# Two batches share one output chunk in a fused attention and gated FFN kernel, with a new instruction order

## The chip, the core and the metric

The kernel runs on one NeuronCore of a Trainium2 chip. The core has a matrix engine (TensorE, in the profile PE, with its weight loads as PEld), a vector engine (VectorE, DVE), a scalar engine (ScalarE, ACT), a general engine (GpSimd, POOL) and a queue engine that only issues DMAs (SyncE, SP). Each engine works through its own instructions strictly in the order in which they were written; semaphores make one engine wait for another. Results of TensorE go to PSUM, everything else on the chip lies in SBUF.

The metric is the device time of one execution in microseconds, as the median of several runs.

## The reference

Eight batches of 576 tokens, eight heads of 64. A causal attention with a forget gate comes first, and its output goes through a feed-forward layer with a gate made by a convolution over the tokens:

```python
scores = scale * np.matmul(q, k.transpose(0, 1, 3, 2))
cum = np.cumsum(np.log(np.clip(f, 0.0001, 1.0)), axis=-1)
decay = cum[:, :, :, None] - cum[:, :, None, :]
scores = np.where(causal, -1000000000.0, scores + decay)
attn = softmax(scores)                         # over the keys
x = np.matmul(attn, v)  -> (8, 576, 512)       # heads side by side
h = np.maximum(x @ w_in, 0.0)                  # 512 -> 1024
conv_out = sum over k of conv_w[k] * h shifted by k - 1 tokens
out = (h * sigmoid(conv_out)) @ w_out          # 1024 -> 512, float32
```

## The kernel before

**Tiles.** The attention is done in 16 half-batches (hb) of four heads, so hb 2b and 2b + 1 make batch b. 576 tokens are four blocks of 128 and a rest of 64. The feed-forward layer takes a batch at a time, in eight blocks (ff) of 128 hidden channels, with all 576 tokens as columns.

**Tasks.** Everything is written as small tasks with short names. `add` gives each its engine, the tasks it comes after, the buffers it takes and those it gives back. The string ORDER (one line, near the top of the file) lists all tasks; `plan.play` writes their instructions in just this order, so ORDER alone sets the order of every engine's queue. `name@ENGINE` picks the engine for tasks that may run on several. The names:

- `q` loads the transposed queries (side 0) or keys (side 1) of an hb with a transposing DMA (L179), into one of four buffers `qk`; hb 0 and 1 are loaded plainly (`ld`) and turned on PE (`tp`). `cl` is a pass over the loaded rows on VectorE (L185; for hb 0 and 1 it is the copy out of PSUM, L171/L173). `rw` puts the decay rows into them by two small DMAs (L201, L202). From hb 8 on `fi` does both with DMAs alone: a blank fill and the decay rows (L193, L195).
- `sd`, `so`, `st`: score matmuls of the diagonal blocks, the other blocks and the 64-token rest (L311, with a mask matmul L319 for hb under 8). `ed`, `eo`, `et`: their exponentials on ScalarE (L352, L369, L331). `md`, `mt`: masks on GpSimd from hb 8 on.
- `v` loads values, `va` casts them (L216, L218). `pv` multiplies probabilities and values (L388, L393); `n` and `m` divide by the sums on VectorE (L402, L404).
- `t` turns the result on PE and `tx` copies it out (L413, L416); for hb 11 to 15 `tx` is a transposing DMA on SP instead (L419).
- `f`: first layer (L428), `r`: relu on ScalarE (L438), `c`, `d`: the convolution on VectorE (L444, L446), `a`: tanh or sigmoid on ScalarE (L449), `g`: the gate on VectorE (L456, L454), which leaves the hidden layer in a buffer `hg`. `h` takes that buffer.
- `o`: second layer. A batch's output is made in chunks of 128 tokens x 512 columns, each 8 matmuls over ff (L463). The chunk of the last 64 tokens is made as two halves of 256 columns, which lie on PSUM partitions 0 to 63 and 64 to 127; that is 16 matmuls of 64 columns of weights (L467). `e` copies chunks out of PSUM to an output buffer `ob`, on ScalarE or VectorE (L473; L478 for the last batch), `s` stores it (L489, L493, L484).

**Buffers.** There are two `hg` buffers, three `ob` buffers (which also take in the weights w_in and w_out at the start, tasks `wi`, `wo`; `wic`, `woc` cast them) and four PSUM tiles `ps`. A task that takes a buffer waits for the task that gave it back.

**Order of the queues.** SP issues nearly all DMAs, in order; an issue that must wait (for a buffer, or as `fi` for the landing of `q`) holds all issues behind it. The same holds for a copy `e` on ScalarE or VectorE which waits for the store that frees its buffer.

The output matmuls before, with the half chunks in the else branch, are these:

```python
if c < 4:
    nc.tensor.matmul(ps[:, 512 * (c % 2):512 * (c % 2 + 1)], hg_of(b, ff)[:, 128 * c:128 * (c + 1)],
                     w_out_f16[:, ff, :], **kw)
else:
    for a in range(2):
        nc.tensor.matmul(ps[64 * a:64 * (a + 1), 0:256], hg_of(b, ff)[:, 512:576],
                         w_out_f16[:, ff, 256 * a:256 * (a + 1)], skip_group_check=True, **kw)
```

Of the kernel before, what the change touches and what calls it, by code (L numbers as in the profile page):

```python
# [7 lines left out]
FP32 = mybir.dt.float32  # L8
# [48 lines left out]
def kernel(  # L57
# [26 lines left out]
    RING, NP, NPT, NVA, NVF, NX, NRC, NXT, NHT, NU, NHG, NOB = 4, 6, 4, 4, 2, 2, 3, 2, 5, 4, 2, 3  # L84
    NPL = 2
    PAIRS = 2
    NCL = 8
    MASK_PE = (0, 1, 2, 3, 4, 5, 6, 7,)
    NPD, NP3 = 2, 2
    TURN_DMA = (11, 12, 13, 14, 15,)  # L90
    CUT, PER, NXB = 14, 7, 18
    VW = D + 2
    LATE = [(b, ff) for b in range(B) for ff in range(8) if b == 7 or b == 6 and ff >= 3]

    cpool = ctx.enter_context(tc.tile_pool(name="const", bufs=1))
    ctx.enter_context(tc.manual_schedule())
# [38 lines left out]
    hg_t = [cpool.tile([128, NFF, S], FP16, name=f"hg{t}") for t in range(NHG)]  # L135
# [547 lines left out]
```

## Time and profile before

| | |
|---|---|
| median of 3 runs | 248.52 us (247.74 to 249.3) |
| the profiled execution's own time | 248.12 us |
| its span (first to last instruction) | 246.4 us |
| TensorE busy | 229.4 us, 93% |
| ScalarE busy | 207.7 us, 84% |
| VectorE busy | 203.8 us, 83% |
| GpSimd busy | 52.1 us, 21% |
| granted TensorE clock | 1.00 throughout |

The span is what the profiler saw of the program; 1.7 us of the execution lie outside it. A busy time is the union of an engine's instructions; matmuls are pipelined, so the rows of PE overlap by some 0.16 us at their ends, and a wait shorter than that hides in a busy PE. Lines such as L428 are those of the program before; in the changed program the same code stands one to eight lines further down.

In the views quoted below, a stretch gives the busy time and the number of instructions for PE, PEld, DVE, ACT and POOL, then the granted clock, the DMA share and GB/s. A piece of the chain of waits gives its start, its length and what the run was held by. A timeline row gives start, length, engine, line, operation, tiles, and in brackets the idle time before it and what ended that.

### The profile page before, as it was taken

The numbers are of one execution on the slowest core, as the hardware profiler recorded it, in microseconds if no ns is written. First come the engines' busy times: TensorE is split into PE (matmuls) and PEld (weight loads), VectorE is DVE, ScalarE is ACT, GpSimd is POOL, SyncE is SP. The second block draws the span as 40 slices with busy tenths as digits, with TensorE's granted clock in tenths as the row PEclk, the third lists the DMA queues.
The fourth block names the chain that finished last, engine by engine and source line by source line (L and its number), as shares of the span: only waits on it lengthen the run. The fifth ranks groups of instructions, "written<-read, shape, count | busy, mean of one in ns | idle before, by whom it ended". The sixth has DMA issues, their size and how long they took to land.

```text
span 246.4 us, 6604 instructions
## 1 busy us (share of the span) xinstructions
PE 229.4 (93%) x2723; PEld 147.6 (60%) x2723; DVE 203.8 (83%) x325; ACT 207.7 (84%) x278; POOL 52.1 (21%) x79
## 2 busy tenths in 40 slices
PE   0798899988999999999999999999989999999993
PEld 0776686566655575586657755685656567445451
DVE  5635068999899999999899889989888889999940
ACT  2764978999989899999889999999989996688733
POOL 8020430011620050021511336030334320000000
PEclk9999999999999999999999999999999999999999
DMA  7999899999899999999999989999899960804335
GB/s 180 331 162 253 260 203 208 189 200 229 263 230 191 212 214 256 230 247 249 217 232 163 243 224 188 240 190 163 240 193 269 200 216 3 179 23 174 106 106 192
DMA packets 120849, 49.70 MB, mean 202 GB/s; under 512 B 109919, under 2 KB 111455, under 8 KB 120819
## 3 DMA queue, kind: packets, MB, share of 16 engines
q1 hardware_dynamic: 120573, 48.91, 92.6%
q8 instruction: 21, 0.34, 0.6%
q10 hardware_dynamic: 246, 0.37, 0.5%
q14 instruction: 9, 0.07, 0.1%
HBM read 21.11 MB, written 10.17 MB: 127 GB/s over the span
## 4 chain that ended last, share of the span: by engine, by line
PE 63%; DMA 13%; DVE 9%; SPq 7%; ACT 4%; issue 2%; ACTq 0%; DVEq 0%
PE ps L428 19%; PE ps L463 18%; PE ps L311 12%; PE ps L388 6%; DMA qk<-in_k_dram 5%; DVE u L446 3%; SPq L179 3%; DMA qk<-in_q_dram 3%; SPq L208 3%; PE ps L467 2%; DMA u<-in_f_dram 2%; PE ps L393 2%; DVE u L444 2%; DMA qk<-image 2%; PE ps L413 2%
## 5 line engine op out<-in xcount | busy, mean ns | idle before, releaser
L428 PE MATMUL ps<-xt,w_in_f 128*128 128x512 f16 (+1 forms) x512 | 69.7, 286 | 0.2 <-DMA xt<-xm 0.2
L369 ACT ACTIVATE pp<-ps 128x1024 f16<-128x1024 f32 x64 | 64.7, 1038 | 3.3 <-PE ps L311 2.1
L311 PE MATMUL ps<-qk 128*128 128x128 bf16 (+2 forms) x576 | 64.0, 240 | 2.9 <-ACT pp L352 0.8
L463 PE MATMUL ps<-w_out_f,hg 128*128 128x512 f16 x256 | 59.7, 379 | 0.0
L444 DVE SCALAR_TENSOR_TENSOR u<-ht,cwt 128x576 f32<-128x576 f16 x64 | 53.3, 846 | 2.2 <-ACT ht L438 2.0
L446 DVE SCALAR_TENSOR_TENSOR u<-ht,cwt,u 128x576 f32<-128x576 f16 x64 | 53.5, 850 | 0.6
L311 PEld LDWEIGHTS <-qk 128*128 128x128 bf16 x576 | 39.0, 98 | 22.0 <-issue 3.5
L449 ACT ACTIVATE hg<-u,cw 128x576 f16<-128x576 f32 x64 | 48.6, 782 | 3.9 <-PE ps L467 1.9
L428 PEld LDWEIGHTS <-w_in_f 128*128 128x128 f16 x512 | 34.2, 98 | 28.9 <-issue 0.5
L438 ACT ACTIVATE ht<-ps 128x576 f16<-128x576 f32 x64 | 41.2, 658 | 5.9 <-PE ps L428 5.1
L463 PEld LDWEIGHTS <-hg 128*128 128x128 f16 x256 | 23.8, 98 | 26.0 <-issue 0.6
L456 DVE SCALAR_TENSOR_TENSOR hg<-hg,ht 128x576 f16<-128x576 f16 x51 | 37.5, 760 | 0.2 <-ACT hg L449 0.2
L355 POOL TENSOR_SCALAR_AFFINE_SELECT pp<-pd 128x1024 f16<-128x1024 f32 x16 | 19.8, 1251 | 47.6 <-ACT pd L352 47.6
L404 DVE TENSOR_TENSOR xm<-ps,rc 128x896 f16<-128x896 f32 (+1 forms) x32 | 23.9, 752 | 1.0 <-DVE rc L402 0.2
L388 PE MATMUL ps<-va,pp 128*128 128x65 f16 x640 | 24.0, 193 | 0.3 <-ACT pp L369 0.3
L388 PEld LDWEIGHTS <-pp 128*128 128x128 f16 x640 | 22.2, 97 | 2.0 <-issue 0.5
L216 POOL CAST va<-vf 128x1024 f16<-128x1024 f32 x9 | 10.8, 1209 | 54.8 <-DMA vf<-in_v_dram 34.2
L352 ACT ACTIVATE pp<-ps 128x1024 f16<-128x1024 f32 x16 | 16.3, 1031 | 1.4 <-PE ps L316 0.8
L473 ACT COPY ob<-ps 128x1024 f32<-128x1024 f32 (+1 forms) x16 | 13.0, 810 | 5.0 <-PE ps L463 1.3
L352 ACT ACTIVATE pd<-ps 128x1024 f32<-128x1024 f32 x16 | 16.4, 1028 | 0.8 <-POOL pt L334 0.5
L402 DVE RECIPROCAL rc<-ps 128x14 f32<-128x14 f32 (+1 forms) x32 | 6.6, 206 | 11.7 <-PE ps L388 7.1
L319 PE MATMUL ps<-mask,ident 128*128 128x512 bf16 (+1 forms) x40 | 14.3, 358 | 1.6 <-ACT qk L171 1.0
(84 smaller groups left out, 187.7 us busy)
## 6 DMA issues: line engine op xcount, KB each, us to landing
vf<-in_v_dram SPq DMA_DIRECT2D x32, 256.0 KB
out_dram<-ob SPq DMA_DIRECT2D x14, 512.0 KB
qk<-blank SPq DMA_DIRECT2D x8, 540.0 KB
ob<-in_moe_w_in_dram SPq DMA_DIRECT2D x4, 512.0 KB
ob<-in_moe_w_out_dram SPq DMA_DIRECT2D x4, 512.0 KB
vf<-in_v_dram SPq DMA_DIRECT2D x8, 128.0 KB
out_dram<-ob SPq DMA_DIRECT2D x4, 256.0 KB
out_dram<-ob SPq DMA_DIRECT2D x15, 64.0 KB
```

The source lines that it names most:

```text
L311: nc.tensor.matmul(o, tk[:, h * S + k0:h * S + k0 + 128], tq[:, h * S + q0:h * S + q0 + n], start=first, stop=last and not by_matmul(hb, h))
L352: nc.scalar.activation(o, ps_of(f"sd{i}").rearrange("p (s c) -> p s c", s=2), AF.Exp, scale=SCALE)
L369: nc.scalar.activation(pair(i)[:, s, 512:1536], ps_of(f"so{i}.{s}"), AF.Exp, scale=SCALE)
L388: nc.tensor.matmul(ps[:, c:c + D + 1], block(hb, h, m, n), va[:, h, m, 0:D + 1], start=(m == 0), stop=(m == n))
L404: nc.vector.tensor_tensor(xm[:, CUT * D * u:CUT * D * u + nj * k * D].rearrange("p (j x d) -> p j x d", x=k, d=D), got[:, :, :, 0:D], r.un ...
L428: nc.tensor.matmul(ps[:, t0:t1], w_in_f16[:, cc, 128 * ff:128 * (ff + 1)], xt[:, cc // 2, x:x + t1 - t0], start=(cc == 0), stop=(cc == NCC ...
L438: nc.scalar.activation(ht_of(b, ff)[:, 2:2 + S], ps_of(f"f{b}.{ff}")[:, 0:S], AF.Relu, scale=1.0 if (b, ff) in LATE else 0.5)
L444: nc.vector.scalar_tensor_tensor(u, ht[:, 1:1 + S], cwt[:, ff, 0:1], ht[:, 2:2 + S], op0=ALU.mult, op1=ALU.add)
L446: nc.vector.scalar_tensor_tensor(u, ht[:, 3:3 + S], cwt[:, ff, 1:2], u, op0=ALU.mult, op1=ALU.add)
L449: nc.scalar.activation(hg_of(b, ff), u_t[slot[f"c{b}.{ff}", "u"]], AF.Sigmoid if (b, ff) in LATE else AF.Tanh, scale=cw[:, ff, 1:2])
L456: nc.vector.scalar_tensor_tensor(hv, hv, 1.0, ht_of(b, ff)[:, 2:2 + S], op0=ALU.add, op1=ALU.mult)
L463: nc.tensor.matmul(ps[:, 512 * (c % 2):512 * (c % 2 + 1)], hg_of(b, ff)[:, 128 * c:128 * (c + 1)], w_out_f16[:, ff, :], **kw)
```

## The change

Three things change together.

**A shared chunk.** The hidden layers of three batches now lie in one tile, `hg_all`, as three neighbouring token ranges: the middle one takes odd batches, the outer two take the even ones in turn. So the last 64 tokens of one batch and the first 64 of its neighbour are 128 adjacent columns. For each pair of batches (2i, 2i + 1) one chunk takes these 128 columns as weights, in 8 full matmuls of 512 columns, and is written as task o(2i+1).4. Even batches have four chunks only. One batch of each pair starts its own four chunks at token 64 (`shift`). The shared chunk needs the gates of both batches; it gives back both buffers. It is copied out once, 128 x 512, and stored by one DMA where the tokens are adjacent in the output and by two DMAs of 64 rows where they are not. The two tasks o.4 and e.2 of each even batch are gone, and so is the store that ScalarE issued at the end.

**Four output buffers.** NOB goes from 3 to 4. Room for it comes from the second mask buffer `p3`, which is now laid over `sel_q`.

**A new ORDER**, in which every engine's queue is rearranged, with other choices of engine for `tx`, `va`, `e` and `woc` (for example tx0 goes from ScalarE to VectorE, e3.2 from VectorE to ScalarE).

```diff
-dca cw ld1 ld0 ld0.0.0 tp0.0.0 dcl ... o7.3.7 s7.1 e7.3@ACT s7.3
+dca cw ld0 ld1 ld0.0.0 tp0.0.0 dcl ... o7.0.7 s7.4 s7.2 s7.3 e7.0@ACT s7.0 e7.1@ACT s7.1
...
-    RING, NP, NPT, NVA, NVF, NX, NRC, NXT, NHT, NU, NHG, NOB = 4, 6, 4, 4, 2, 2, 3, 2, 5, 4, 2, 3
+    RING, NP, NPT, NVA, NVF, NX, NRC, NXT, NHT, NU, NHG, NOB = 4, 6, 4, 4, 2, 2, 3, 2, 5, 4, 3, 4
...
-    p3_t = [cpool.tile([128, HH, SL], FP32, name=f"p3{t}") for t in range(NP3)]
+    p3_t = [cpool.tile([128, HH, SL], FP32, name="p30"), sel_q.bitcast(FP32)]
...
-    hg_t = [cpool.tile([128, NFF, S], FP16, name=f"hg{t}") for t in range(NHG)]
+    hg_all = cpool.tile([128, NFF, NHG * S], FP16, name="hg")
...
     def hg_of(b, ff):
-        return hg_t[slot[f"h{b}", "hg"]][:, ff, :]
+        t = 1 if b % 2 else 2 * slot[f"h{b}", "he"]
+        return hg_all[:, ff, S * t:S * (t + 1)]
...
+    def low(b):
+        return slot[f"h{b - b % 2}", "he"] == 0
+
+    def shift(b):
+        return 0 if low(b) == (b % 2 == 0) else S - 512
+
+    def shared(b, ff):
+        return hg_all[:, ff, 512:640] if low(b) else hg_all[:, ff, 2 * S - SL:2 * S + SL]
+
     def ffn2(b, first, c, ffs):
         ps = ps_of(first)
         for ff in ffs:
-            kw = dict(start=(ff == 0), stop=(ff == NFF - 1))
-            if c < 4:
-                nc.tensor.matmul(ps[:, 512 * (c % 2):512 * (c % 2 + 1)], hg_of(b, ff)[:, 128 * c:128 * (c + 1)],
-                                 w_out_f16[:, ff, :], **kw)
-            else:
-                for a in range(2):
-                    nc.tensor.matmul(ps[64 * a:64 * (a + 1), 0:256], hg_of(b, ff)[:, 512:576],
-                                     w_out_f16[:, ff, 256 * a:256 * (a + 1)], skip_group_check=True, **kw)
+            t = shift(b) + 128 * c
+            w = hg_of(b, ff)[:, t:t + 128] if c < 4 else shared(b, ff)
+            nc.tensor.matmul(ps[:, 512 * (c % 2):512 * (c % 2 + 1)], w, w_out_f16[:, ff, :], start=(ff == 0), stop=(ff == NFF - 1))
...
-        else:
-            for a in range(2):
-                e = nc.scalar if a and b == B - 1 else nc.sync
-                e.dma_start(outf[r:r + SL, 256 * a:256 * (a + 1)], ob[64 * a:64 * (a + 1), 0, 0:256])
+        elif shift(b):
+            nc.sync.dma_start(outf[b * S - SL:b * S + SL, :], ob[:, 0, :])
+        else:
+            nc.sync.dma_start(outf[b * S + 512:(b + 1) * S, :], ob[0:SL, 0, :])
+            nc.sync.dma_start(outf[(b - 1) * S:(b - 1) * S + SL, :], ob[SL:128, 0, :])
...
-                add(f"h{b}", "ACT", [f"d{b}.{ff}"], lambda: None, take=["hg"])
+                add(f"h{b}", "ACT", [f"d{b}.{ff}"], lambda: None, take=["ho" if b % 2 else "he"])
...
-            for c in range(5):
+            for c in range(4 + b % 2):
...
-                    behind=[f"o{b}.{c - 1}"] if c else [], give=[("hg", f"h{b}")] if c == 4 else [])
+                    behind=[f"o{b}.{c - 1}"] if c else [], give=[("he", f"h{b - 1}"), ("ho", f"h{b}")] if c == 4 else [])
```

Three places of the new order matter below. The first is SP's queue early in the program, around the first transposing loads: qk0 to qk3 are the buffers of hb 4, 1 (or 5), 2 and 3, image holds the decay rows, vf1 the values of batch 1. Before:

```order
L503 DMA ob0_127<-in_moe_w_in_dram 128x2x512
L201 DMA qk2_87<-image_65 1x2304
L202 DMA qk2_87<-image_65 2x2304
L179 DMA_TRANSPOSE qk0_85<-in_q_dram 128x2304
L179 DMA_TRANSPOSE qk3_88<-in_q_dram 128x2304
L179 DMA_TRANSPOSE qk0_85<-in_k_dram 128x2304
L179 DMA_TRANSPOSE qk3_88<-in_k_dram 128x2304
L208 DMA vf1_90<-in_v_dram 128x8x64 x2
L201 DMA qk0_85<-image_65 1x2304
L202 DMA qk0_85<-image_65 2x2304
```

And after:

```order
L510 DMA ob3_128<-in_moe_w_in_dram 128x2x512
L202 DMA qk2_87<-image_65 1x2304
L203 DMA qk2_87<-image_65 2x2304
L180 DMA_TRANSPOSE qk3_88<-in_q_dram 128x2304
L180 DMA_TRANSPOSE qk3_88<-in_k_dram 128x2304
L180 DMA_TRANSPOSE qk0_85<-in_k_dram 128x2304
L209 DMA vf1_90<-in_v_dram 128x8x64
L209 DMA vf1_90<-in_v_dram 64x8x64
L209 DMA vf1_90<-in_v_dram 128x8x64
L202 DMA qk3_88<-image_65 1x2304
L203 DMA qk3_88<-image_65 2x2304
L209 DMA vf1_90<-in_v_dram 128x8x64 x2
```

Hb 3 (qk3) is now loaded ahead of hb 4 (qk0), hb 4's queries have moved to the row behind the last one shown, and the last piece of w_in has a buffer of its own.

The second place is SP's queue between the load of hb 11's turned result (tx11) and hb 14's loads (qk2); qk3 is hb 15's. Before:

```order
L419 DMA_TRANSPOSE xt1_115<-xm1_110 128x9x128
L179 DMA_TRANSPOSE qk3_88<-in_q_dram 128x2304
L179 DMA_TRANSPOSE qk3_88<-in_k_dram 128x2304
L489 DMA out_0_dram<-ob2_129 128x2x512
L208 DMA vf0_89<-in_v_dram 64x8x64
L193 DMA qk3_88<-blank_66 60x4x1152
L195 DMA qk3_88<-image_65 4x2x2304
L493 DMA out_0_dram<-ob0_127 64x256 x2
L179 DMA_TRANSPOSE qk2_87<-in_k_dram 128x2304
```

And after:

```order
L495 DMA out_0_dram<-ob2_127 128x2x512
L209 DMA vf0_89<-in_v_dram 128x8x64 x4
L420 DMA_TRANSPOSE xt1_114<-xm0_108 128x9x128
L180 DMA_TRANSPOSE qk3_88<-in_k_dram 128x2304
L180 DMA_TRANSPOSE qk3_88<-in_q_dram 128x2304
L495 DMA out_0_dram<-ob1_126 128x2x512
L209 DMA vf0_89<-in_v_dram 64x8x64
L194 DMA qk3_88<-blank_66 60x4x1152
L196 DMA qk3_88<-image_65 4x2x2304
L180 DMA_TRANSPOSE qk2_87<-in_k_dram 128x2304
```

The small store of batch 2's last 64 tokens (s2.2), which stood behind hb 15's fill, is gone; batch 2's store s2.1 stands ahead of tx11.

The third place is VectorE's queue at the norms of the last two half-batches, whose results batch 7's first layer needs: xm0 and xm1 are hb 15 and 14 before, and 14 is xm1 and 15 xm0 after as well. Before:

```order
L404 TENSOR_TENSOR xm0_109<-ps0_130,rc2_113 128x256
L402 RECIPROCAL rc0_111<-ps1_131 128x14
L446 SCALAR_TENSOR_TENSOR u3_124<-ht1_117,cwt_72,u3_124 128x576
L404 TENSOR_TENSOR xm1_110<-ps1_131,rc0_111 128x896
L402 RECIPROCAL rc1_112<-ps3_133 128x4
L404 TENSOR_TENSOR xm1_110<-ps3_133,rc1_112 128x256
L444 SCALAR_TENSOR_TENSOR u1_122<-ht3_119,cwt_72 128x576
```

And after:

```order
L405 TENSOR_TENSOR xm1_109<-ps3_132,rc2_112 128x896
L448 SCALAR_TENSOR_TENSOR u3_123<-ht0_115,cwt_72,u3_123 128x576
L448 SCALAR_TENSOR_TENSOR u0_120<-ht4_119,cwt_72,u0_120 128x576
L403 RECIPROCAL rc0_110<-ps2_131 128x4
L458 SCALAR_TENSOR_TENSOR hg_124<-hg_124,ht3_118 128x576
L405 TENSOR_TENSOR xm1_109<-ps2_131,rc0_110 128x256
L403 RECIPROCAL rc1_111<-ps3_132 128x4
L446 SCALAR_TENSOR_TENSOR u1_121<-ht3_118,cwt_72 128x576
L456 TENSOR_TENSOR hg_124<-hg_124,ht1_116 128x576
L405 TENSOR_TENSOR xm0_108<-ps3_132,rc1_111 128x256
```

Hb 15 was finished ahead of hb 14; now its last part comes last, behind a convolution pass and a gate.

More of the change, by code (lines that the diff above doesn't have):

```diff
@@ L544 @@
                 add(f"tp{hb}.{p}.{side}", "PE", [got[p, side]], lambda hb=hb, p=p, side=side: turn_qk(hb, p, side),
-                    take=["ps"], give=[("hg", f"ld{hb}")] if (p, side) == (1, 1) else [],
+                    take=["ps"], give=[("he", f"ld{hb}")] if (p, side) == (1, 1) else [],
                     behind=[f"tp{hb}.{x}.{y}" for x, y in parts] [:2 * p + side])
@@ L625 @@
         wo = [f"woc{j}" for j in range(4)]
+        before = [f"g{b - 1}.{ff}" for ff in range(NFF)]
         if last:
@@ L628 @@
                 for c in range(NKB):
-                    add(f"o{b}.{c}.{ff}", "PE", [f"g{b}.{ff}"] + (wo if ff == 0 else []),
+                    add(f"o{b}.{c}.{ff}", "PE", [f"g{b}.{ff}"] + (before if c == 4 and ff == 0 else []) + (wo if ff == 0 else []),
                         lambda b=b, c=c, ff=ff: ffn2(b, f"o{b}.{c & ~1}.0", c, [ff]),
@@ L645 @@
             continue
-        for a in range(3):
+        for a in range(2 + b % 2):
             first, made = f"o{b}.{2 * a}", f"o{b}.{min(2 * a + 1, 4)}"
```

23 lines of the change are left out of this document (12 added, 11 removed).

## The prediction

> **What bounds the kernel now.** I read the head of the page first, then stretches of the span, then the chain that ended last, then the instructions at the places where TensorE stands still. The head:
>
> ```profile
> span 246.4 us, 6604 instructions
> PE 229.4 (93%) x2723; PEld 147.6 (60%) x2723; DVE 203.8 (83%) x325; ACT 207.7 (84%) x278; POOL 52.1 (21%) x79
> ```
>
> TensorE is busy 93% of the span, so 17.0 us of it are idle. The stretches (length, then busy time of PE, PEld, DVE, ACT and POOL, clock, DMA share) say where those lie:
>
> ```profile
> 0.00:27.00 27.00, 17.41 (x194) 14.24 (x194) 13.54 (x36) 15.18 (x15) 7.07 (x34) 1.00 1.03 230
> 27.00:42.00 15.00, 14.90 (x238) 11.03 (x239) 7.72 (x14) 12.40 (x16) 4.69 (x5) 1.00 1.10 223
> 42.00:66.00 24.00, 22.02 (x297) 14.93 (x295) 23.86 (x36) 23.75 (x34) 4.08 (x4) 1.00 1.08 225
> 66.00:165.00 99.00, 98.74 (x1230) 63.77 (x1229) 92.87 (x139) 93.00 (x127) 25.30 (x25) 1.00 1.06 219
> 165.00:183.00 18.00, 17.07 (x206) 10.78 (x204) 15.59 (x25) 16.90 (x25) 4.33 (x6) 1.00 1.05 200
> 183.00:242.30 59.30, 59.24 (x568) 32.85 (x566) 50.18 (x80) 45.86 (x66) 6.60 (x6) 1.00 0.58 143
> 242.30:246.40 4.10, 0.00 (x0) 0.00 (x0) 0.00 (x0) 0.56 (x1) 0.00 (x0) 1.00 0.63 221
> ```
>
> Idle PE is 9.6 us in the loading phase, 2.0 between 42 and 66, 0.26 in the next 99 us, 0.93 from 165 to 183, and 4.1 after the last matmul. Between 42 and 66 the bound is VectorE and ScalarE (23.86 and 23.75 of 24). From 66 on it is TensorE, at full clock: PE work removed there shortens the run one for one, and nothing else does but the waits inside it.
>
> **The shared chunk.** The chain of waits names both kinds of output matmul on the path, and a first-layer group beside them:
>
> ```profile
> 122.50 1.00 PE ps L467 x16
> ...
> 124.47 0.98 PE ps L428 x8
> ...
> 128.05 1.73 PE ps L463 x8
> ...
> 236.16 1.43 PE ps L467 x24
> ...
> 240.50 0.56 PE ps L467 x8
> ```
>
> A batch's last 64 tokens cost 16 half-width matmuls (L467), about 0.995 us; eight batches give 6 x 0.995 + 1.43 + 0.56 = 7.96 us. The change puts a full chunk of 8 matmuls (1.73) in their place, once for two batches: 4 x 1.73 = 6.92. That is 1.04 us less, and all of it lies in the stretch where PE is the bound. **Term: -1.04.** Half a full chunk would be 0.865, so the gain is the 0.13 us that each batch pays on entering and leaving the half-width mode.
>
> The Trainium skill speaks against a gain here: its page "TensorE: Matmul & The Clock Gate" (Measured speedup vs the span model) has matmuls packed side by side take the time of one, plus some 4 ns for each further tile. By that rule the halves were already packed for nothing, eight pairs in a batch would cost what half a chunk costs, and this term would be near 0 instead of -1.04. The trace agrees on the packing itself and differs by that 0.13 us.
>
> The copies out of PSUM change in shape:
>
> ```profile
> L473 ACT COPY ob<-ps 128x256 f32<-128x256 f32 x5 | 1.9, 372 | 1.9 <-PE ps L467 1.2 <-ACT hg L449 0.7
> L478 ACT COPY ob<-ps 128x512 f32<-128x512 f32 x4 | 2.2, 587 | 3.0 <-PE ps L463 3.0
> L473 DVE COPY ob<-ps 128x256 f32<-128x256 f32 x2 | 0.9, 426 | 2.5 <-ACT p L331 1.4 <-DMA out_dram<-ob 1.1
> ```
>
> ScalarE gives up five of 0.372 and gets three of 0.587 (-0.1 us); VectorE gives up two of 0.426. The pairs of half stores become one or two stores for each two batches on SP. I cost all this at nothing: PE covers it from 66 on, with 6 us spare on either engine up to 165 and 9 to 13 after it. Without that cover it would be a gain of under 1 us. The third buffer of the hidden layer and the second mask buffer laid over sel_q (last read by batch 0's first half) add no instruction.
>
> **Waits in the stretch 165 to 183.** The three idle places of PE, and what VectorE waited for:
>
> ```profile
> 167.93 2.61 PE L428 MATMUL ps<-xt,w_in_f 128*128 128x512 f16 x20 [0.25 <-DMA xt<-xm]
> ...
> 180.23 0.72 PE L311 MATMUL ps<-qk 128*128 128x64 bf16 x12 [0.39 <-DMA qk<-blank]
> ...
> 180.77 0.42 DVE L473 COPY ob<-ps 128x256 f32<-128x256 f32 x1 [1.11 <-DMA out_dram<-ob]
> ...
> 181.24 0.61 PE L311 MATMUL ps<-qk 128*128 128x128 bf16 x8 [0.29 <-DVE ob L473]
> ```
>
> and the chain behind them on SP:
>
> ```profile
> 168.10 6.34 DMA qk<-in_k_dram
> ...
> 174.52 0.90 SPq L193
> ...
> 176.21 0.56 SPq L493
> 176.82 3.86 DMA out_dram<-ob
> ```
>
> SP stands at the blank fill of half-batch (hb) 15 until its key load has landed; the store s2.2 is queued behind it, and batch 3's last copy (e3.2, on VectorE) needs that buffer. In the new order this copy is ScalarE's, takes the buffer of s2.1, which stands ahead of tx11, and s2.2 is gone: the 0.29 goes. The other two hang on SP's line of tx11, hb 15's two loads and its fill, which starts at hb 11's last norm, and on hb 15's first and hb 14's next user:
>
> ```profile
> 163.25 0.42 DVE L404 TENSOR_TENSOR xm<-ps,rc 128x256 f16<-128x256 f32 x1
> ```
> ```profile
> 191.72 1.49 PE L311 MATMUL ps<-qk 128*128 128x128 bf16 x20
> ```
>
> From that norm's end (163.67) f5.0 could run on after 4.3 us (167.93) and hb 15's first scores after 16.6 (180.23). In the new order the PE work that stands between, counted by the same rows (1.73 for an output chunk, 0.98 for a first-layer group, 0.44 for a score group), is about 4.5 us to f5.0, so the 0.25 goes, and about 16.1 us to hb 15's first scores, so the 0.39 mostly stays. Hb 14's loads and fill are next in that line; their user came 11.5 us after hb 15's (191.72) and now has 9.6 us of work ahead of it, with one store less in the line: that is what comes late next, by some tenths. Bounds: -0.93 and +1. **Term: -0.5**, the two waits that lose their cause.
>
> **The early part.** Its rows:
>
> ```profile
> 22.64 4.37 DMA qk<-image
> ...
> 33.07 6.23 DMA qk<-in_q_dram
> ```
> ```profile
> 36.11 1.12 ACT L416 COPY xt<-ps 128x1152 f16<-128x1152 f16 x1 [1.27 <-PE ps L413]
> ...
> 38.99 0.65 ACT L438 ACTIVATE ht<-ps 128x576 f16<-128x576 f32 x1 [0.84 <-PE ps L428]
> ```
> ```profile
> 37.50 0.75 DVE L416 COPY xt<-ps 128x1152 f16<-128x1152 f16 x1
> 39.33 0.88 DVE L185 TENSOR_SCALAR qk<-qk,lim 128x2304 uint16<-128x2304 uint16 x1 [1.07 <-DMA qk<-in_q_dram]
> 40.12 0.81 DVE L444 SCALAR_TENSOR_TENSOR u<-ht,cwt 128x576 f32<-128x576 f16 x1
> ...
> 51.37 0.68 DVE L216 CAST va<-vf 128x1024 f16<-128x1024 f32 x1
> ```
>
> pv0.0 moves into the wait for hb 1's decay rows (22.64 to 27.01), so PE has 1 us less to do after it; I cost that at nothing, since after 28 ScalarE's exponentials are late next, and one small one (et1) is now among them. tx0 moves from ScalarE (1.12) to VectorE (0.75), between m1.0 and n1.1, so t1, tx1 and f0.0 come about 0.9 later. Against that, hb 3's loads now lead SP's queue, the fourth buffer lets w_in's four pieces go out without a wait, and the 1.07 us that VectorE waited at 39.33 goes. VectorE nets -0.3, ScalarE +0.9 of lateness, less the 1.12 and plus a cast of va3.0 (about 1.0). Both engines are full from 42 to 66, so what is late there stays late. Bounds: -2.0 (all PE idle of that stretch goes) and +1.7 (0.9 and the cast, no relief). **Term: +0.5**, nearer to VectorE's value, the fuller engine.
>
> **Elsewhere.** From 66 to 165 the nearest row is 0.26 us of idle; a new order can take that away or, if it runs ScalarE as close as between 42 and 66 (2.0 in 24) for 12 us more, add 1.0. I take +0.2. At the end:
>
> ```profile
> 242.24 1.00 SPq L484 DMA_DIRECT2D out_dram<-ob  x2
> 242.28 0.58 ACT L478 COPY ob<-ps 128x512 f32<-128x512 f32 x1
> ```
>
> one copy (0.58) and two store issues follow the last matmul. Now e7.0 waits for it and e7.1 stands behind e7.0 on ScalarE: +0.58 at most; three of the five last stores are out by then, and the last goes alone: -0.5 at best. I take +0.2.
>
> **Sum:** -1.04 - 0.5 + 0.5 + 0.2 + 0.2 = -0.64 us. The profiled execution took 248.12 (span 246.4 and 1.7 around it), 0.4 under the median 248.52; the same step on the median gives 247.9.
>
> **Rivals.** (1) The halves were free: the 0.13 a batch is latency that the full chunk shows as well. The x24 in 1.43 (0.06 each, two batches run together) speaks a little for it, the equal 0.99 in quite different neighbourhoods against. Then -0.64 + 1.04 = +0.4: 248.9. This is the page's rule above, by its own road.
> (2) The first stage comes free: PE's 2.0 us of idle between 42 and 66 go instead of the +0.5. For it: the wait at 39.33 is gone, hb 3 and 4 have their rows before use. Against: two engines full there. 247.9 - 2.5 = 245.4.
> (3) Slower: VectorE stands at hb 4's query clamp. Its load, the first of the four before, is now issued behind hb 3's decay rows and two value loads, which wait for cl3.1. By the rows: tx1 ends near 39.2, two clamps of 0.8, then rows and values on SP, the load at about 43.4. VectorE reaches the clamp near 51.1, after va2.0 (at 51.37 before). It decides if the load takes over 7.7 us; the one quoted took 6.2. All engines wait behind VectorE there, so each further us is one of time; with the DMA share at 1.08, 4 us more are possible: 251.9.
> A smaller one is inside the forecast. The load of hb 15 for the last batch:
>
> ```profile
> 208.01 0.42 DVE L404 TENSOR_TENSOR xm<-ps,rc 128x256 f16<-128x256 f32 x1
> ```
> ```profile
> 208.50 3.65 SPq L419 DMA_TRANSPOSE xt<-xm  x2
> ```
> ```profile
> 215.40 1.85 PE L428 MATMUL ps<-xt,w_in_f 128*128 128x512 f16 x13
> ```
>
> had 3.25 us from issue to use. Now hb 15 comes last, and 3 x 1.73 + 2 x 0.98 = 7.15 us of PE work separate its last product from f7.0, of which norms queued on VectorE and SP's issue take some 5.1: about 2 us are left, and 0 to 1.2 may be lost.
>
> **How the numbers follow.** Chances: forecast 0.50, (1) 0.14, (2) 0.19, (3) 0.17. About 1% is what a measurement can tell: under 246.0 is faster, over 251.0 slower. So faster 0.19, same 0.64, slower 0.17. The forecast's own range is 246.5 to 249.5; to leave out no more than 2 in 10 it has to reach into (2) and (3): 244.7 to 251.6.
>
> **What would show it.** Right: PE's output group has 288 matmuls of 128x512 and none of 64 columns, about 6.9 us where the tails had 8; no wait of a copy on a store; VectorE without a wait on a query load before c0.0; f0.0 near 38.7; under 0.3 us of PE idle from 66 to 160. Wrong: PE idle between 42 and 66 under 1 or over 4, a wait of over 1 us at f7.0, or more than 5 us after the last matmul.

## The result and the profile after

| | before | after |
|---|---|---|
| median | 248.62 us (20 runs, 247.04 to 250.29) | 247.12 us (20 runs, 245.78 to 251.76) |
| ratio after / before | | 0.9939, 95% interval 0.9914 to 0.9963 |
| the profiled execution | 248.12 us, span 246.4 | 245.78 us, span 244.1 |

The change made the kernel 1.5 us faster (0.9 to 2.1): the interval stays clear of no change, but the gain is under 1%. The profiled execution of the changed kernel is its fastest run, 1.3 us under its median, which is to be kept in mind in everything read from it. The head of its page:

```profile
span 244.1 us, 6385 instructions
PE 226.9 (93%) x2627; PEld 145.0 (59%) x2627; DVE 205.1 (84%) x323; ACT 206.9 (85%) x278; POOL 52.9 (22%) x77
```

TensorE's busy time fell by 2.5 us (229.4 to 226.9), its idle time rose by 0.2 (17.0 to 17.2). The whole gain of the profile, 2.3 us, is thus work and short waits inside the busy time; the longer waits only changed places. The stretches of the changed kernel (length, then busy time of PE, PEld, DVE, ACT and POOL, clock, DMA share and GB/s) show where to:

```profile
0.00:27.00 27.00, 19.42 (x241) 16.34 (x242) 15.06 (x38) 16.34 (x16) 8.04 (x35) 1.00 1.02 238
27.00:42.00 15.00, 14.23 (x205) 9.96 (x203) 8.49 (x14) 12.17 (x16) 3.84 (x4) 1.00 1.13 223
42.00:66.00 24.00, 20.67 (x286) 13.95 (x283) 23.56 (x36) 23.18 (x34) 6.04 (x5) 1.00 1.07 237
66.00:165.00 99.00, 98.99 (x1208) 63.80 (x1206) 93.44 (x138) 95.34 (x131) 23.15 (x23) 1.00 1.08 218
165.00:183.00 18.00, 18.00 (x219) 11.28 (x217) 15.62 (x23) 16.99 (x25) 6.96 (x8) 1.00 1.07 227
183.00:238.70 55.70, 55.56 (x481) 29.69 (x479) 48.63 (x77) 41.82 (x61) 4.91 (x7) 1.00 0.50 132
238.70:244.10 5.40, 0.00 (x0) 0.00 (x0) 0.27 (x1) 1.07 (x2) 0.00 (x0) 0.96 0.65 222
```

| PE idle, us | before | after |
|---|---|---|
| 0 to 27 | 9.59 | 7.58 |
| 27 to 42 | 0.10 | 0.77 |
| 42 to 66 | 1.98 | 3.33 |
| 66 to 165 | 0.26 | 0.01 |
| 165 to 183 | 0.93 | 0.00 |
| 183 to the last matmul | 0.06 | 0.14 |
| after the last matmul | 4.1 | 5.4 |

The 2.0 us won in the first stage are all given back by 66 us (sum 11.67 before, 11.68 after). The middle is now without a gap, and the end is 1.3 us longer. The two output lines of before, and the one of after (busy time, mean ns):

```profile
L463 PE MATMUL ps<-w_out_f,hg 128*128 128x512 f16 x256 | 59.7, 379 | 0.0
L467 PE MATMUL ps<-w_out_f,hg 128*64 128x256 f16 x128 | 8.5, 275 | 0.0
```
```profile
L474 PE MATMUL ps<-w_out_f,hg 128*128 128x512 f16 x288 | 66.8, 379 | 0.0
```

68.2 us of output matmuls became 66.8. That is 1.4 of the 2.5 us, and not all of it is work: the rows overlap at their ends, and there are fewer groups now. Busy time is 1.6 to 2.5 us lower than before in the five profiles with the new order and the shared chunk that are at full clock throughout, but only 0.5 to 1.0 in the three with the order before and the shared chunk (below). What the rest of the 2.5 is, no run shows.

The tasks of the first stage, by the chain that ended last (start, length, what it was held by):

```profile
22.71 3.01 DMA qk<-image
...
42.19 7.33 DMA qk<-in_q_dram
...
49.55 0.88 DVE qk L186
```

The decay rows of hb 1 were issued as in before, at 22.7 us, and landed after 3.01 us instead of 4.37. The start of batch 0's first layer, f0.0, is this row before,

```profile
37.73 2.21 PE L428 MATMUL ps<-xt,w_in_f 128*128 128x512 f16 x16
```

and this one after:

```profile
36.77 2.21 PE L429 MATMUL ps<-xt,w_in_f 128*128 128x512 f16 x16
```

The query load that the third rival is about went out at 42.19 and landed at 49.52, just as its clamp on VectorE (L186) was due.

The end, as a timeline (start, length, engine, line; in brackets the idle time before and what ended it):

```profile
236.32 0.69 DVE L484 COPY ob<-ps 128x512 f32<-128x512 f32 x1 [2.10 <-PE ps L474]
237.04 0.47 SPq L499 DMA_DIRECT2D out_dram<-ob  x1
237.56 0.59 SPq L500 DMA_DIRECT2D out_dram<-ob  x1
237.66 0.58 ACT L484 COPY ob<-ps 128x512 f32<-128x512 f32 x1 [3.40 <-issue]
238.27 2.31 SPq L490 DMA_DIRECT2D out_dram<-ob  x4
238.28 0.69 DVE L484 COPY ob<-ps 128x512 f32<-128x512 f32 x1 [1.27 <-ACT ob L484]
238.69 1.07 ACT L484 COPY ob<-ps 128x512 f32<-128x512 f32 x2 [0.45 <-PE ps L474]
```

The last matmul ends at 238.7. Two copies follow it in a row on ScalarE, and the issues of the four stores of 256 KB last until 240.58, 1.9 us after the last matmul; before, the last issue (L484, 242.24 for 1.00) ended 1.0 us after it. VectorE's copy at 238.28 had waited 1.27 us for ScalarE's copy into the same buffer.

### The profile page after: what moved, and what is told of

The parts are those of the page before. It is cut to its first block, busy times and chain, and to the rows that moved or that the text cites. A ratio compares the mean times of both kernels' runs of the same rounds, so it can differ in the third digit from the quotient of the medians.

```text
span 244.1 us, 6385 instructions
## 1 busy us (share of the span) xinstructions
PE 226.9 (93%) x2627; PEld 145.0 (59%) x2627; DVE 205.1 (84%) x323; ACT 206.9 (85%) x278; POOL 52.9 (22%) x77
## 4 chain that ended last, share of the span: by engine, by line
PE 78%; DVE 7%; DMA 6%; ACT 4%; issue 1%; ACTq 1%; SPq 1%; DVEq 0%
PE ps L474 24%; PE ps L429 20%; PE ps L312 15%; PE ps L389 7%; DMA qk<-in_q_dram 3%; PE ps L320 3%; PE ps L394 3%; PE ps L166 2%; PE ps L414 2%; DVE u L446 2%; ACT pp L370 2%; DMA pd<-in_moe_conv_w_dram 2%; DVE u L448 2%; DVE qk L186 1%; DMA qk<-image 1%
## 5 line engine op out<-in xcount | busy, mean ns | idle before, releaser
L474 PE MATMUL ps<-w_out_f,hg 128*128 128x512 f16 x288 | 66.8, 379 | 0.0
L446 DVE SCALAR_TENSOR_TENSOR u<-ht,cwt 128x576 f32<-128x576 f16 x64 | 52.7, 837 | 3.6 <-ACT ht L440 3.4
L474 PEld LDWEIGHTS <-hg 128*128 128x128 f16 x288 | 26.9, 98 | 28.8
L458 DVE SCALAR_TENSOR_TENSOR hg<-hg,ht 128x576 f16<-128x576 f16 x51 | 38.7, 771 | 0.6 <-ACT hg L451 0.5
L389 PE MATMUL ps<-va,pp 128*128 128x65 f16 x640 | 24.8, 193 | 1.1 <-DVE va L217 1.0
L389 PEld LDWEIGHTS <-pp 128*128 128x128 f16 x640 | 22.6, 97 | 3.7 <-DVE va L217 1.3
L217 POOL CAST va<-vf 128x1024 f16<-128x1024 f32 x8 | 10.0, 1252 | 32.1 <-DMA vf<-in_v_dram 27.8
```

The source lines that it names most:

```text
L389: nc.tensor.matmul(ps[:, c:c + D + 1], block(hb, h, m, n), va[:, h, m, 0:D + 1], start=(m == 0), stop=(m == n))
L446: nc.vector.scalar_tensor_tensor(u, ht[:, 1:1 + S], cwt[:, ff, 0:1], ht[:, 2:2 + S], op0=ALU.mult, op1=ALU.add)
L458: nc.vector.scalar_tensor_tensor(hv, hv, 1.0, ht_of(b, ff)[:, 2:2 + S], op0=ALU.add, op1=ALU.mult)
L474: nc.tensor.matmul(ps[:, 512 * (c % 2):512 * (c % 2 + 1)], w, w_out_f16[:, ff, :], start=(ff == 0), stop=(ff == NFF - 1))
```

## The experiments

Three things were changed at once, so the first runs take them apart. All ratios are to the kernel before on the same chip in the same call; with 7 to 12 runs each their intervals are about 0.3% to either side, or 0.8 us, and two ratios have to differ by some 0.45% to be told apart. Each profile is of one run, which lies anywhere from 2.2 us under its kernel's median (order before, shared chunk, three buffers) to 1.9 us over it (new order, end sorted by tile). A table of PE's idle time in each profile stands behind the runs.

### The order before, with the shared chunk

The changed kernel's code, three output buffers, and the order before without the tasks that are gone:

```diff
-NHG, NOB = 4, 6, 4, 4, 2, 2, 3, 2, 5, 4, 3, 4
+NHG, NOB = 4, 6, 4, 4, 2, 2, 3, 2, 5, 4, 3, 3
 ORDER: that of before, without o0.4 e0.2 s0.2 o2.4 e2.2 s2.2 o4.4 e4.2 s4.2 o6.4 e6.2 s6.2
```

> The old order with the shared chunk and three output buffers: the half-chunk tasks of the even batches are struck from the order, nothing else is moved. Theory A (the sum of the prediction): 1.0 to 1.2 us of PE work less, and batch 3's last copy finds its buffer free, so the 0.29 of PE idle at 181 goes: 1.0 to 1.5 us faster than before (ratio 0.994 to 0.996). Theory B (the halves were free, the gain comes from the new order): ratio 0.999 to 1.001. Under A the early rows and the end stay as before (first batch-1 first-layer matmul near 64.8, 4.2 us after the last matmul).

Measured: 249.70 us against 249.57, ratio 0.9989 (0.9958 to 1.0020). By the time alone the shared chunk would be worth nothing, as theory B has it, though the interval reaches down to theory A's 0.996. The trace, of the fastest of the twelve runs, tells more. The stretch from 165 to 183 us:

```profile
165.00:183.00 18.00, 17.95 (x204) 11.26 (x203) 16.80 (x26) 17.17 (x26) 4.40 (x6) 1.00 1.03 200
```

PE's idle time there is 0.05 where it was 0.93, with the order before and three buffers, and no copy waits for a store in it. For the 0.29 the rotation of the buffers is the cause: a half-width chunk had taken a whole output buffer for a quarter of its bytes; without it e3.2 gets the buffer that s2.1 gives back, and s2.1 stands ahead of hb 15's fill in this order too. The other two waits, 0.25 and 0.39, were for DMAs. The fill that the 0.39 hung on was issued 5.0 us after hb 15's second load here (168.09 to 173.10) and 6.4 us before (168.10 to 174.52). It is 4.95 to 5.3 us in all eleven kernels with the shared chunk and 6.0 to 6.5 in the three with half chunks; no run shows why.

TensorE does not wait less in all, though. From 66 to 165 us it is idle for 1.49 us in this profile and was for 0.26 before, so from 66 to 183 the sum is 1.54 against 1.19 (0.91 and 1.23 in the two further runs with this order and the shared chunk). The longest of the new gaps is a wait for a relu:

```profile
153.74 3.61 PE L474 MATMUL ps<-w_out_f,hg 128*128 128x512 f16 x16 [0.56 <-ACT ht L440]
```

The same with four buffers:

```diff
-NHG, NOB = 4, 6, 4, 4, 2, 2, 3, 2, 5, 4, 3, 3
+NHG, NOB = 4, 6, 4, 4, 2, 2, 3, 2, 5, 4, 3, 4
```

> The same with four output buffers. Theory A: the buffer that batch 3's last copy needs is already free with three, so the fourth adds nothing: within 0.2 us of the run with three. Theory C (the fourth buffer is what removed the waits from 165 to 183): 0.5 us or more faster than with three.

Measured: 247.66 us, 0.9924 (0.9889 to 0.9959). The order before, with shared chunk and fourth buffer, is as fast as the changed kernel (0.9939 and, below, 0.9927). In the time, the new order is worth nothing that can be measured. The fourth buffer came out at 1.6 us here (0.5 to 2.8), the number of theory C; its cause is another, since the waits from 165 to 183 were gone with three buffers already.

### The fourth buffer alone

The kernel before, with its order and its half chunks:

```diff
-NHG, NOB = 4, 6, 4, 4, 2, 2, 3, 2, 5, 4, 2, 3
+NHG, NOB = 4, 6, 4, 4, 2, 2, 3, 2, 5, 4, 2, 4
-    p3_t = [cpool.tile([128, HH, SL], FP32, name=f"p3{t}") for t in range(NP3)]
+    p3_t = [cpool.tile([128, HH, SL], FP32, name="p30"), sel_q.bitcast(FP32)]
```

> The kernel before, with its own order and its half-width tails, and only the fourth output buffer. Theory C (the fourth buffer does more than end two waits of copies on stores: weight pieces and stores go out earlier, and the early stage gets its data sooner): a ratio to before of 0.992 to 0.996, 1.0 to 2.0 us faster. Rival A (the account of the prediction: the buffer ends the two waits of copies on stores, 0.3 to 0.7 us, and nothing else): 0.997 to 0.999.

Measured: 249.34 us against 250.28, 0.9970 (0.9937 to 1.0002): at the edge between the two ranges, and no more than 1.6 us. Its stretch from 165 to 183:

```profile
165.00:183.00 18.00, 17.14 (x210) 11.05 (x209) 16.49 (x26) 17.29 (x26) 3.82 (x6) 1.00 1.02 197
```

Still 0.86 us idle, but the 0.29 for a store is not among them: e3.2 has the buffer of s2.1 here too, so either change ends that wait. What is left are the two waits for DMAs:

```profile
169.13 2.61 PE L428 MATMUL ps<-xt,w_in_f 128*128 128x512 f16 x20 [0.47 <-DMA xt<-xm]
181.43 1.17 PE L311 MATMUL ps<-qk 128*128 128x64 bf16 x20 [0.38 <-DMA qk<-blank]
```

They are gone in every profile with the shared chunk. Between this run and the one before it only the chunk and the chip differ, and 0.9970 against 0.9924 is 0.46% or 1.15 us for it, with an uncertainty as large.

### The new order with the half chunks

The kernel before with four buffers and the new order, into which the four removed chunks, copies and stores are put back behind their neighbours:

```diff
-... o0.3 d1.5 m4.0 ...
+... o0.3 o0.4 e0.2@ACT d1.5 m4.0 ...
-... e2.1@ACT so23.0 ...
+... e2.1@ACT e2.2@ACT so23.0 ...
```

> The new order and four buffers with the old half-width chunks: the tails of batches 0, 2, 4 and 6 are put back behind their own chunks, two hidden buffers. Theory A: loses the 1.0 to 1.2 us of PE work again, ratio to before about 0.998 to 0.999 where the full change has 0.994. Theory B: as fast as the full change, 0.994.

Measured: 251.15 us, 1.0083 (1.0052 to 1.0113), outside what either theory said: 1.4% or 3.6 us slower than the changed kernel, over twice what the matmuls cost. PE's busy time of this kernel:

```profile
PE 229.6 (92%) x2723; PEld 147.9 (59%) x2723; DVE 205.7 (82%) x323; ACT 208.0 (83%) x282; POOL 52.6 (21%) x77
```

2.7 us more busy time than the changed kernel, and 2.6 more idle. Where it is idle says little: 0.80 us between 66 and 165 and 1.22 from 183 to 236 stand against 0.01 and 0.10 in the first profile of the changed kernel, but against 1.56 and 0.85 in its second (below). The order was made for five copies per pair of batches and has to place a sixth here, on a ScalarE that is full; that this is what costs the time is argued, not shown. An order fits the code it was searched for, so this run does not price the half chunks.

### The new order with three buffers

```diff
-NHG, NOB = 4, 6, 4, 4, 2, 2, 3, 2, 5, 4, 3, 4
+NHG, NOB = 4, 6, 4, 4, 2, 2, 3, 2, 5, 4, 3, 3
```

> The new order and the shared chunk with three output buffers. In this order two stores (s2.0, s3.2) are issued only behind the last transposing loads, so two buffers are held from batch 2 on. Theory A: batch 3's last copy on ScalarE then has to wait for the store issued directly ahead of it, about 4 us as one store took before (3.86), with relu and exponentials behind it: 2 to 4 us slower than the full change, ratio 1.00 to 1.01. Theory D (the buffer count does not matter, the search could have done with three): 0.994.

ORDER is that of the changed kernel, letter for letter; the same copies now share three buffers.

Measured: 248.49 us, 0.9958 (0.9934 to 0.9981), 0.2% to 0.3% slower than with four buffers, inside the uncertainty. Theory A is out: the copy that it is about began at 176.19 without a wait. Theory D's 0.994 lies in the interval. So the fourth buffer came out at 1.6, 0.75 and 0.5 to 0.8 us in three settings. The sign is always the same, and each size is close to its uncertainty. All that the traces show of it is a wait of VectorE's copy for a store, 1.11 us in the kernel before (0.29 for TensorE) and 0.31 in this one, and none with four buffers; what else it acts through is open.

### The changed kernel again

> The changed kernel once more, so that the three kernels beside it have it on their own chip. Expected: a ratio to before of 0.992 to 0.996, as it has been (0.9939).

Measured: 248.52 us against 250.28, 0.9927 (0.9899 to 0.9956), as expected. Its profile, at 246.5 us of span 2.4 longer than that of the first, is worth more than the ratio. Up to 66 us it is 0.7 better. Then the chain that ended last goes through this:

```profile
96.01 6.58 DMA qk<-in_q_dram
...
102.60 5.43 DMA qk<-blank
```

The fill of a half-batch cannot be issued before its query load has landed, and here it landed late: PE waited 1.0 us for it at 107 us:

```profile
108.39 0.61 PE L312 MATMUL ps<-qk 128*128 128x128 bf16 x8 [1.00 <-DMA qk<-blank]
```

The first profile had no wait there. The stretch without a gap from 66 to 165 us belongs to that execution and to some others, not to the kernel.

### The query load of hb 4, early

```diff
-... q4.1 v1.0 so4.1 ... d0.4 q4.0 va2.0@DVE ...
+... q4.1 q4.0 v1.0 so4.1 ... d0.4 va2.0@DVE ...
```

> The changed kernel with the query load of head 0 of head batch 4 issued directly behind that of head 1, as in the order before. Theory S (the 3.3 us that TensorE stands still from 42 to 66 us come from the chain through ScalarE and VectorE, and the load landed just as its clamp came up): the same as the changed kernel within 0.4 us, with 2.8 to 3.8 us of TensorE idle time from 42 to 66 us. Rival R (the third rival of the prediction, at work in part: VectorE is held there by the query load): 0.5 to 1.5 us faster than the changed kernel, idle time under 2.6 us.

Measured: 249.31 us, 0.9977 (0.9945 to 1.0008), and 5.46 us of PE idle from 42 to 66: both expectations missed, it is slower by 0.4% to 0.5%. The waits of that stretch (total, times, longest):

```profile
DVE va L217 <- DMA vf<-in_v_dram: 2.3, 1, 2.3
PE ps L312 <- DMA qk<-image: 2.1, 1, 2.1
PE ps L389 <- DVE va L217: 1.8, 1, 1.8
```

The same last row in the changed kernel:

```profile
PE ps L389 <- DVE va L217: 1.0, 1, 1.0
```

SP's queue shows why (start and length of the issue). With the early load:

```profile
38.29 2.64 SPq L180 DMA_TRANSPOSE qk<-in_q_dram  x1
...
43.06 0.52 SPq L202 DMA_DIRECT2D qk<-image  x1
...
44.34 1.10 SPq L209 DMA_DIRECT2D vf<-in_v_dram  x2
```

and in the changed kernel:

```profile
40.00 0.39 SPq L202 DMA_DIRECT2D qk<-image  x1
...
41.13 1.02 SPq L209 DMA_DIRECT2D vf<-in_v_dram  x2
42.19 7.17 SPq L180 DMA_TRANSPOSE qk<-in_q_dram  x2
```

The transposing load holds SP for 2.64 us, and what stands behind it, decay rows and values, goes out 3.1 and 3.2 us later. Putting the load late was right: it was the one with time to spare, though only just, and not in every execution (see the third rival below).

### The end of the kernel, four ways

Two edits in the last 3 us of the changed kernel:

```diff
-... o7.0.5 e7.3@DVE o7.0.6 o7.1.7 o7.0.7 s7.4 ...
+... o7.0.5 e7.3@ACT o7.0.6 o7.0.7 o7.1.7 s7.4 ...
```

> The changed kernel with two edits in its last 3 us: the last matmul of chunk 0 of batch 7 goes ahead of the last one of chunk 1, and chunk 3 is copied by ScalarE behind chunk 2 instead of by VectorE, which waited 1.27 us for ScalarE's copy into the same buffer. Theory T (the time from the last matmul to the end is set by when the last copies finish, so the new end costs about 0.8 us): 0.5 to 1.0 us less than the changed kernel, and 4.4 to 4.9 us from the last matmul's end to the end of the span in place of 5.4. Rival U (five stores of 256 KB are still to go out when the last matmul ends, and their bytes set the end): unchanged within 0.3 us.

Measured: 248.48 us, 0.9916 (0.9885 to 0.9947), 0.1% below the changed kernel on the same chip, inside the uncertainty. From the last matmul to the end:

```profile
240.14:245.50 5.36, 0.00 (x0) 0.00 (x0) 0.00 (x0) 1.11 (x3) 0.00 (x0) 0.90 0.68 227
```

5.36 us where it was 5.4. VectorE's wait is gone and the end is not a bit nearer: theory T is out, and rival U's number came true.

Sorted by chunk, each copied and stored as it is finished:

```diff
-... o7.0.3 o7.4.0 ... o7.4.7 o7.0.4 o7.3.6 o7.1.5 o7.2.6 e7.4@DVE ... s7.0 e7.1@ACT s7.1
+... o7.2.6 o7.2.7 e7.2@ACT s7.2 o7.3.6 o7.3.7 e7.3@ACT s7.3 o7.0.6 o7.0.7 e7.0@ACT s7.0 o7.1.6 o7.1.7 e7.1@ACT s7.1 o7.4.0 ... o7.4.7 e7.4@DVE s7.4
```

> The changed kernel with its last matmuls sorted by chunk: chunk 2 of batch 7 is finished first, then 3, 0 and 1, and the shared chunk with its eight matmuls last; each chunk is copied and stored as it is finished, the first four by ScalarE. Theory U (in the changed kernel four stores of 256 KB and two of 128 KB, about 1.28 MB, start after 238.3 us, while the last matmul ends at 238.7, and their bytes and issues set the end, 5.4 us later): the span ends 3.4 to 4.0 us after the last matmul in place of 5.4, and the time is 1.2 to 2.0 us less than the changed kernel's, a ratio to before of 0.985 to 0.989. Rival V (the end is set by what follows the last copy, about 4.3 us in the changed kernel and in the run with the two edits in its last 3 us, whatever was stored ahead of it): the last copy ends 0.7 us after the last matmul, so 5.0 us, and 0.4 us less than the changed kernel.

Measured: 248.54 us against 249.29, 0.9957 (0.9922 to 0.9992), 0.2% to 0.3% slower than the changed kernel. PE in the last 6 us:

```profile
239.51 1.02 PE L474 MATMUL ps<-w_out_f,hg 128*128 128x512 f16 x4 [0.67 <-ACT ob L484]
241.27 2.32 PE L474 MATMUL ps<-w_out_f,hg 128*128 128x512 f16 x10 [0.73 <-ACT ob L484]
```

The edit itself made these two waits: chunks 2 and 3 lie in one PSUM tile, and so do 0 and 1. A matmul into the second half of a tile waits until the copy out of the first half is done, 0.7 us each time. The end itself did shorten, to 4.6 us after the last matmul: less than rival V's 5.0, more than theory U's 4.0.

The same end on the order before with shared chunk and four buffers:

> The order before with the shared chunk and four output buffers, and the same sorted end as the kernel beside it. Theory U: the span ends 3.4 to 4.0 us after the last matmul (4.5 before the edit), 0.5 to 1.1 us less than the same kernel without the edit (0.9924), so a ratio to before of 0.988 to 0.991. Rival V: as without the edit within 0.3 us. Theory E (the new order is worth nothing by itself; shared chunk and buffer carry the gain): within 0.8 us of the new order with the sorted end. Rival G (the new order is worth the 0.8 us of its early stage, and only its end gave it back): 0.8 us or more slower than the new order with the sorted end.

Measured: 249.51 us, 0.9985 (0.9948 to 1.0022). With the same two stalls, 3.65 us from the last matmul to the end (4.5 without the edit), as theory U had it; the sum of both is a loss. It is 0.3% slower than the new order with the same end, less than the uncertainty: E and G are not told apart by this pair.

Sorted by tile, so that no matmul waits:

```diff
+... o7.2.6 o7.3.6 o7.2.7 o7.3.7 e7.2@ACT s7.2 e7.3@ACT s7.3 o7.4.0 ... o7.4.7 e7.4@DVE s7.4 o7.0.6 o7.1.6 o7.0.7 o7.1.7 e7.0@ACT s7.0 e7.1@ACT s7.1
```

> The changed kernel with its end sorted by PSUM tile instead of by chunk: chunks 2 and 3 of batch 7, which lie in one tile, are both finished before either is copied, then the shared chunk, then chunks 0 and 1, so that no matmul writes a tile while a copy of it is due (the two stalls of 0.84 and 0.89 us in the run sorted by chunk). Theory U' (what is stored late sets the end, and the stalls were the price of the sorting by chunk alone): no stall of TensorE over 0.2 us in the last 8 us, the span ends 3.9 to 4.5 us after the last matmul in place of 5.4, 0.9 to 1.4 us less than the changed kernel, a ratio to before of 0.987 to 0.991. Rival W (the end follows the last copy whatever was stored before it, 4.3 us behind it in the changed kernel): 5.2 us or more after the last matmul, as fast as the changed kernel within 0.3 us.

Measured: 247.58 us against 248.95, 0.9928 (0.9897 to 0.9959), the changed kernel's ratio. The stalls are gone, but the end is 5.2 us after the last matmul, as rival W had it:

```profile
241.69 0.69 DVE L484 COPY ob<-ps 128x512 f32<-128x512 f32 x1 [3.62 <-PE ps L474]
242.41 0.48 SPq L499 DMA_DIRECT2D out_dram<-ob  x1
242.56 1.07 ACT L484 COPY ob<-ps 128x512 f32<-128x512 f32 x2 [1.52 <-PE ps L474]
242.95 0.58 SPq L500 DMA_DIRECT2D out_dram<-ob  x1
243.63 1.02 SPq L490 DMA_DIRECT2D out_dram<-ob  x2
```

Two stores of 256 KB had been issued by 241.41, 1.1 us before the last matmul's end, which did not help. But SP's last issue ends at 244.65, 2.1 us after the last matmul. Seven ends side by side, in us after the last matmul:

| | last copy ends | last issue ends | span ends | last issue to end |
|---|---|---|---|---|
| before | 0.6 | 1.0 | 4.2 | 3.2 |
| order before, shared, four buffers | 0.6 | 1.3 | 4.5 | 3.2 |
| the same, sorted by chunk | 0.7 | 1.1 | 3.65 | 2.6 |
| changed kernel | 1.1 | 1.9 | 5.4 | 3.5 |
| two edits | 1.1 | 1.9 | 5.4 | 3.4 |
| new order, sorted by chunk | 0.7 | 1.9 | 4.6 | 2.7 |
| new order, sorted by tile | 1.1 | 2.1 | 5.2 | 3.0 |

The end stands 2.6 to 3.5 us behind the last issue, the more the more was stored late, and the edits left that issue where it was. The new order puts it 0.6 to 0.9 us later than the order before, and the rows show two reasons: two copies in a row behind the last matmul, and in the sorted ends the shared chunk's store, which is two issues there (L499, L500, 0.48 and 0.58) and one in the order before (L497, 0.33). In the changed kernel itself those two issues are done before the last matmul, so there the first reason is what is left. SP in the kernel with the order before, shared chunk and four buffers, the shared chunk's store first:

```profile
239.85 0.33 SPq L497 DMA_DIRECT2D out_dram<-ob  x1
240.65 0.84 SPq L490 DMA_DIRECT2D out_dram<-ob  x2
```

This reading was made after the runs, and no run moved the last issue alone.

### The new start on the order before

The first 78 tasks of the new ORDER, then all others in the order before, with the end sorted by chunk:

> As the kernel beside it with the old order and the sorted end, but the first 78 steps of the order are the new ones, up to the first normalization of attention group 0, so that TensorE has the first weighted sum to do while the padded query rows of the second pair of heads land. Theory G (the early part of the new order is worth about 0.8 us, and the old order loses less from 42 to 66 us): 0.4 to 1.0 us less than with the old start, a ratio to before of 0.985 to 0.989. Rival (the start's gain in the profile of the changed kernel was the luck of one landing, 3.0 us where 4.4 was before): the same as with the old start within 0.3 us.

Measured: 250.10 us, 1.0014 (0.9977 to 1.0051); with the old start it was 0.9985. No gain from the start: theory G is out by its own numbers, and the difference of 0.3% the other way is within the uncertainty. Its profile is of a run 2.1 us above the median and is left out of what follows.

### Idle time of PE in all profiles

| us | 0 to 66 | 66 to 165 | 165 to 183 |
|---|---|---|---|
| before | 11.67 | 0.26 | 0.93 |
| order before, four buffers | 12.74 | 0.41 | 0.86 |
| order before, shared | 10.81 | 1.49 | 0.05 |
| order before, shared, four buffers | 10.76 | 0.86 | 0.05 |
| the same, sorted by chunk | 11.99 | 1.18 | 0.05 |
| changed kernel | 11.68 | 0.01 | 0.00 |
| changed kernel again | 10.99 | 1.56 | 0.00 |
| two edits at the end | 12.66 | 0.01 | 0.00 |
| new order, sorted by chunk | 12.54 | 0.01 | 0.00 |
| new order, sorted by tile | 13.02 | 2.09 | 0.00 |
| new order, half chunks | 12.66 | 0.80 | 0.21 |
| new order, three buffers | 13.48 | 0.01 | 0.00 |
| new order, early query load | 13.41 | 0.01 | 0.00 |

In two of them (new order sorted by chunk, and with three buffers) the granted clock was 0.97 in the first 66 us, so a little of what they show there is that.

## Why the prediction was right, step by step

The time came out at 247.12 for a forecast of 247.9, in the range and within 1%. Of the change itself, 1.5 us, the forecast had 0.64. The shared chunk was right; of the other terms the sizes and some of the causes were not, and that their errors balanced is luck.

- **Shared chunk, -1.04: right.** The output rows show -1.4, with some overlap in it, and the two pairs of runs that differ in nothing else but the chunk show -1.15 with four buffers and -0.3 with three, each about 1 us uncertain. Rival (1), that the halves were free, is spoken against by the rows; the run with three buffers alone would not have excluded it. The rule of the Trainium skill beside it ("TensorE: Matmul & The Clock Gate", Measured speedup vs the span model) does not hold here to the last tenth: the eight full matmuls of a pair of batches take less than its 32 packed ones (7.1 us, 66.8 less 59.7, against 8.5 for all four pairs).
- **Waits from 165 to 183, -0.5: the size too small, the cause right in part.** All 0.93 went. The 0.29 went as the prediction had it, with the buffer of s2.1 and without s2.2; but the new order, to which the prediction gave it, is not needed for that, since the shared chunk alone does it and so does the fourth buffer alone. The 0.25, given to more PE work ahead of f5.0 in the new order, goes with the shared chunk alone as well. The step that failed is "the 0.39 mostly stays". It set PE work against a load that takes as long as before, and hb 15's load came to its fill in 5.0 us instead of 6.4, as in every kernel with the shared chunk. What the prediction also lacked is that a gap can move: with the order before and the shared chunk TensorE waits about as long from 66 to 183 us as before (0.91 to 1.54 us for 1.19). With the new order and the shared chunk it is 0.01 in five of seven profiles, and 1.56 and 2.09 in the two others.
- **The early part, +0.5: 0.0 in this profile, by luck.** f0.0 began at 36.77 and not near 38.7, but the rows of hb 1 landed 1.3 us sooner in it, at 25.72 for 27.01. The run with the two edits at its end has the same early part, and there they landed at 27.01 as well:

```profile
22.89 4.12 DMA qk<-image
...
37.89 2.21 PE L429 MATMUL ps<-xt,w_in_f 128*128 128x512 f16 x16
```

  With the landing alike, f0.0 is 0.2 us later than before (37.73), so the step of "t1, tx1 and f0.0 come about 0.9 later" failed; the idle time up to 66 us is 12.66 for 11.67, 1.0 more. Five profiles with the new order, the shared chunk and four buffers (the changed kernel twice, the three with another end) average 12.2 us of it, five with the order before 11.6: the forecast's size, but either five scatter by 2 us. The price was paid where it was looked for: 3.33 us idle from 42 to 66, with VectorE and ScalarE at 23.56 and 23.18 of 24. Rival (2) is out.
- **Rival (3)** lies on the edge that the prediction drew. The load took 7.33 us, and VectorE did not wait for it. In the runs sorted by tile and with three buffers it took 7.89 and 8.20 us, and VectorE's clamp waited:

```profile
50.95 0.88 DVE L186 TENSOR_SCALAR qk<-qk,lim 128x2304 uint16<-128x2304 uint16 x1 [0.70 <-DMA qk<-in_q_dram]
51.58 0.88 DVE L186 TENSOR_SCALAR qk<-qk,lim 128x2304 uint16<-128x2304 uint16 x1 [0.99 <-DMA qk<-in_q_dram]
```

  The load less the wait puts the limit near 7.2 us, where the prediction had 7.7. TensorE's idle time from 42 to 66 is 3.95 and 3.96 us there (the second at a granted clock of 0.93) in place of 3.33. So it costs up to 1 us in some executions, not 4, and the cure, an early load, is worse than the wait.
- **66 to 165, +0.2:** -0.25 in the profile and in most others of the new order with the shared chunk, +1.3 and +1.8 in two. What the prediction did not see is the place at 107 to 111 us: the fill behind the late query load.
- **The end, +0.2: wrong, +1.3.** The step that failed is "three of the five last stores are out by then, and the last goes alone". At the last matmul's end (238.7) only the shared chunk's two issues were done; the four of 256 KB began at 238.27. The end of the order before grew by 0.3 with the shared chunk and four buffers (4.2 to 4.5), the new order adds 0.9. "More than 5 us after the last matmul" was named as what would show it wrong.
- **Hb 15's load (0 to 1.2 us lost):** no wait at f7.0.

Summed by the profile, busy time -2.5, early part 0.0, 66 to 165 -0.25, 165 to 183 -0.93, up to the last matmul +0.1, the end +1.3: -2.3, the difference of the spans. The medians give -1.5; the profile of after was its fastest run.

By the time, the change as a whole is its first two parts. The order before with shared chunk and four buffers gives 0.9924, the changed kernel 0.9939 and 0.9927. The new order, in most executions, closes the last gaps between 66 and 183 us, and its profiles pay for it before 66 and at the end. No kernel tried beats the changed one by more than the uncertainty; the lowest ratio is 0.9916.

## What to carry to other kernels

A removed task is also a removed turn of every buffer it took: count that before crediting a fourth buffer or a new order with a wait that ends. When a gap closes, add up the idle time around it: it may only have moved. When an order is searched anew, run the old order with the new code; here it did as well. At the end of a kernel, look at when the last store is issued, not only at when the last matmul or copy ends, and do not let a copy of half a tile stand between matmuls into the other half.

## What the runs showed of the hardware beside this

- Two executions of the same program had spans of 244.1 and 246.5 us, at full clock in both. 1.0 us of that is the wait at 107 us for the fill behind one late load. The same small row DMAs, issued at 22.6 to 23.2 us, took from 3.01 to 4.37 us in six profiles.
- A transposing load occupies the queue that issues it for microseconds: 2.64 us for one, 7.17 for two. Moved ahead by 3.9 us, one of them cost 2.3 us of waiting for values and 2.1 us for decay rows, which stood behind it in the queue.
